# Attention followed by a mixture-of-experts layer: tokens sorted by expert on chip, gathered in slot tiles, and scattered back

## The chip, the core and the metric

The kernel runs on one core of a Trainium2 chip. The metric is the device time of one execution in microseconds (us); lower is better. Five engines work from queues of their own, each in program order: TensorE (PE in the profile; its weight loads are PEld), VectorE (DVE), ScalarE (ACT), GpSimd (POOL), and SyncE (SP), which here only issues transfers. POOL issues transfers too. All transfers share 16 DMA engines.

## What is computed

The reference has two layers. The first is attention with normalised queries and keys, 8 batches x 12 heads, 448 tokens, head size 64. Its output, as rows of 768 numbers, is the input of the second layer: a dense feed-forward network (FFN) for every token, plus the FFN of the one expert of eight that the token's gate picks, weighted by the gate's probability.

```python
x = np.ascontiguousarray(attn_out.transpose(0, 2, 1, 3)).reshape(B * S, H * D)   # 3584 x 768
h_dense = np.maximum(x @ w1_dense, 0.0)          # 768 -> 512
y_dense = h_dense @ w2_dense                     # 512 -> 768
logits = x @ w_gate
expert_idx = np.argmax(logits, axis=1)
probs = softmax(logits)
gate_w = probs[np.arange(N), expert_idx]
for e in range(E):
    mask = expert_idx == e
    h = np.maximum(x[mask] @ w1[e], 0.0)
    y_moe[mask] = gate_w[mask, None] * (h @ w2[e])
return y_dense + y_moe
```

## The kernel before

**Attention** goes over 48 steps t: 8 batches of 6 pairs of heads. The loop at the end of the first `with` block writes the order out by hand. In step t it loads and squares inputs for t+6 (`norm_ahead`, with GP = 3 pairs to one load), normalises t+3, computes `scores` for t+1 and `attend` for t in four parts, transposes the result of t-1 (`xtrans`), transposes q and k of t+2, and ends with `divide(t)`. A step has 52 TensorE instructions of the matmul kind: 8 scores (L137), 32 attend (L150), 8 transposes of q and k (L121) and 4 of the result (L168). ScalarE does the exponentials (`ex`, L139), the copy of the transposed result into `xc` (L170), and once in GP steps `rnorm` (L102 and L103, a logarithm and an exponential), each of which is preceded by a load of its function table. VectorE does the sums of squares (L96), the normalising products (L111), the copies of the transposes (L126, L128) and `divide`. POOL does the squares (L95) and issues the loads of v (`vr`, L84), which VectorE spreads into `va` (L87). SP issues the loads of q and k (L77).

`xc` holds the whole result, transposed (768 numbers of a token lie across partitions), for all 3584 tokens. No token order is changed anywhere.

**The second layer** begins with the gate: 192 matmuls of 8 columns (L220), then a few VectorE operations that leave in `ge` the gate's weight of the chosen expert and zero for the others. Then comes a loop over nine sets of weights: the dense one and the eight experts (e from -1 to 7). The weights `w1t` (L250) and `w2t` (L252) are loaded by POOL into two buffers each. Every set is applied to all 8 batches of 448 tokens: 24 matmuls into `hp` (L258), ScalarE's relu into `ht` (L261), 32 matmuls into `yps` (L267), and VectorE adds the result into `yacc`, multiplied by `ge` (L274; L272 copies for the dense set). An expert thus also runs on the tokens that are not its own, with a factor of zero. With the last expert, the output of a batch is stored as soon as it is complete.

## Time and profile before

| | |
|---|---|
| runs of the kernel before | 1080.33 us median of 3 (1079.74 to 1081.66) |
| the profiled execution | 1080.28 us, its span 1078.2 us |
| instructions | 15442, of them 6720 matmuls |
| busy share of the span | PE 91%, PEld 60%, DVE 47%, ACT 37%, POOL 12% |
| mean granted TensorE clock | 0.911 of full speed |
| moved by the DMA engines | 53.68 MB, mean 50 GB/s |

The span runs from the first to the last instruction. A busy share is a mean over two stages of different kinds, so the stages have to be looked at apart. Matmuls are pipelined: one starts before the record of the previous one ends, so the time of a matmul in a stream is read from a group's length divided by its count, and not from its mean. The granted clock is a share of 2.4 GHz; 0.5 is 1.2 GHz. In the trace, an arrow behind an idle time names what the instruction waited for.

### The profile page before, as it was taken

How to read it: one execution, taken by the hardware profiler on the slowest of the kernel's cores; microseconds unless marked ns; L12 is line 12 of the kernel's file. 1: busy time of each engine (PE TensorE's matmuls, PEld its weight loads, DVE VectorE, ACT ScalarE, POOL GpSimd, SP SyncE). 2: the span in 40 equal slices, each digit the busy share in tenths (PEclk: the TensorE clock that was granted, in tenths of full speed). 3: DMA queues.
4: the chain of work that ended last, by engine and by line, in shares of the span. 5: the costliest groups of instructions: out<-in, count | busy, mean ns of one | idle time of the engine just before them, and what ended most of it. 6: DMA issues, size and time to landing. Idle time of an engine off the chain costs nothing.

```text
span 1078.2 us, 15442 instructions
## 1 busy us (share of the span) xinstructions
PE 985.4 (91%) x6720; PEld 651.4 (60%) x6720; DVE 505.5 (47%) x716; ACT 395.5 (37%) x593; POOL 129.4 (12%) x129
## 2 busy tenths in 40 slices
PE   0579888888897999999999999999999999999996
PEld 0246555555555866666666666666666666666664
DVE  2866657666642333443444334433444344433443
ACT  1577777867765022222222222222222222222221
POOL 4744242342200000000000000000000000000000
PEclk9999956656657699999999999999999999999999
DMA  9964424513000000300300300300301202100334
GB/s 187 195 145 78 105 76 81 125 52 101 3 1 3 1 1 1 59 1 1 60 1 1 59 1 1 59 1 1 59 1 15 45 1 31 29 1 1 121 136 153
DMA packets 46899, 53.68 MB, mean 50 GB/s; under 512 B 2160, under 2 KB 45936, under 8 KB 45936
## 3 DMA queue, kind: packets, MB, share of 16 engines
q0 software_dynamic: 23472, 19.67, 12.7%
q1 hardware_dynamic: 23360, 33.03, 10.7%
q8 instruction: 52, 0.85, 0.3%
q14 instruction: 15, 0.12, 0.0%
HBM read 61.37 MB, written 11.01 MB: 67 GB/s over the span
## 4 chain that ended last, share of the span: by engine, by line
PE 81%; ACT 9%; DMA 4%; DVE 3%; issue 1%; POOL 0%; SPq 0%; ACTq 0%; POOLq 0%; DVEq 0%
PE yps L267 35%; PE hp L258 31%; PE av L150 6%; PE ps L137 6%; ACT ex L139 5%; DMA t<-in_k_dram 3%; PE ps L121 2%; PE lp L220 2%; DVE y L111 2%; PE ps L168 1%; ACT L102 1%; ACT L103 1%; DMA vr<-in_v_dram 1%; DVE ssq L96 1%; ACT xc L170 0%
## 5 line engine op out<-in xcount | busy, mean ns | idle before, releaser
L274 DVE SCALAR_TENSOR_TENSOR yacc<-yps,ge,yacc 112x768 f32<-112x768 f32 x256 | 260.5, 1018 | 362.9 <-PE yps L267 362.9
L267 PE MATMUL yps<-w2t,ht 128*112 128x384 bf16 x2304 | 386.2, 326 | 0.0
L261 ACT ACTIVATE ht<-hp 128x448 bf16<-128x448 f32 x288 | 156.5, 543 | 540.5 <-PE hp L258 540.5
L267 PEld LDWEIGHTS <-ht 128*112 128x112 bf16 x2304 | 299.5, 130 | 81.0
L258 PE MATMUL hp<-xc,w1t 128*128 128x448 bf16 x1728 | 340.7, 354 | 0.0
L258 PEld LDWEIGHTS <-w1t 128*128 128x128 bf16 x1728 | 169.7, 98 | 153.0 <-issue 2.4
L139 ACT ACTIVATE ex<-ps 112x896 bf16<-112x896 f32 x192 | 166.2, 915 | 46.1 <-PE ps L137 45.6
L137 PE MATMUL ps<-y 64*112 64x448 bf16 x384 | 127.3, 551 | 36.2 <-ACT ex L139 35.9
L95 POOL TENSOR_TENSOR sq<-t 112x512 f32<-112x512 f32 x96 | 105.8, 1124 | 141.6 <-DMA t<-in_q_dram 107.5
L150 PEld LDWEIGHTS <-ex 112*128 112x128 bf16 x1536 | 84.0, 123 | 57.3 <-issue 52.8
L150 PE MATMUL av<-va,ex 112*128 112x65 bf16 x1536 | 103.6, 234 | 3.6 <-DVE xa L160 3.6
L121 PE MATMUL ps<-ident,y 112*128 112x112 bf16 x384 | 46.4, 281 | 39.7 <-DVE y L111 33.1
L137 PEld LDWEIGHTS <-y 64*112 64x112 bf16 x384 | 37.8, 160 | 72.9 <-issue 66.6
L96 DVE TENSOR_REDUCE ssq<-sq 112x8 f32<-112x512 f32 x96 | 61.8, 676 | 25.5 <-POOL sq L95 25.2
L111 DVE TENSOR_TENSOR y<-t,r 112x512 bf16<-112x512 f32 x96 | 72.4, 763 | 0.0
L250 POOL DMA_DIRECT2D w1t<-in_moe_w_dram x8 | 6.6, 830 | 527.4 <-PE hp L258 527.4
L121 PEld LDWEIGHTS <-y 112*128 112x128 bf16 x384 | 33.0, 133 | 48.8 <-DVE y L111 35.4
L126 DVE TENSOR_SCALAR y<-ps,gqk 128x448 bf16<-128x448 bf16 x48 | 21.5, 448 | 68.4 <-PE ps L121 68.4
L272 DVE COPY yacc<-yps 112x768 f32<-112x768 f32 x32 | 30.6, 957 | 43.5 <-PE yps L267 43.5
L170 ACT COPY xc<-ps 128x448 bf16<-128x448 bf16 x48 | 25.5, 532 | 26.2 <-PE ps L168 26.1
L160 DVE TENSOR_TENSOR xa<-av,inv 128x512 bf16<-128x512 f32 x48 | 32.8, 684 | 0.2
L168 PE MATMUL ps<-ident,xa 128*128 128x128 bf16 x192 | 27.5, 292 | 1.0 <-DVE xa L160 1.0
(35 smaller groups left out, 165.9 us busy)
## 6 DMA issues: line engine op xcount, KB each, us to landing
t<-in_q_dram SPq DMA_DIRECT2D x16, 672.0 KB, 6.3
t<-in_k_dram SPq DMA_DIRECT2D x16, 672.0 KB, 7.6
out_dram<-yacc SPq DMA_DIRECT2D x8, 1344.0 KB, 6.2
w1t<-in_moe_w_dram POOLq DMA_DIRECT2D x8, 768.0 KB, 7.4
w2t<-in_moe_w_dram POOLq DMA_DIRECT2D x8, 768.0 KB, 9.0
vr<-in_v_dram POOLq DMA_DIRECT2D x8, 672.0 KB, 7.4
w1t<-in_moe_w_dense_dram POOLq DMA_DIRECT2D x1, 768.0 KB, 9.8
w2t<-in_moe_w_dense_dram POOLq DMA_DIRECT2D x1, 768.0 KB, 10.7
```

What stands on the lines that cost most here:

```text
L95: nc.gpsimd.tensor_mul(sq, x, x)
L96: nc.vector.tensor_reduce(ssqs[g][:, n, 2 * i * JJ:(2 * i + 2) * JJ], sq.rearrange("p h (j d) -> p (h j) d", d=D), AX.X, ALU.add)
L111: nc.vector.tensor_mul(y.rearrange("p j h d -> p h j d"), x.rearrange("p h (j d) -> p h j d", d=D), rs[g][:, n, 2 * i * JJ:(2 * i + 2) * J ...
L121: nc.tensor.transpose(ps[:, j * SC:(j + 1) * SC], xn[name, t][:, j].rearrange("p h d -> p (h d)"), ident[:SC, :SC])
L137: nc.tensor.matmul(ps[:, hh, :S], qkT["k", t][d0:d0 + D, j * SC:(j + 1) * SC], qkT["q", t][d0:d0 + D, :], start=True, stop=True)
L139: nc.scalar.activation(exs[t][:, j], ps[:, :, :S], AF.Exp, scale=scale)
L150: nc.tensor.matmul(av[t][:, hh, mi * De:(mi + 1) * De], exs[t][:, j, hh, QC[mi]:QC[mi] + P], vas[b][:, 2 * pr + hh, j, :De], start=(j == 0 ...
L168: nc.tensor.transpose(ps[:, QC[mi]:QC[mi] + P], xnats[t][:, mi].rearrange("p h d -> p (h d)"), ident)
L258: nc.tensor.matmul(hp, w1t[:, kk, ff * P:(ff + 1) * P], xc[:, kk, b * S:(b + 1) * S], start=(kk == 0), stop=(kk == KD - 1))
L261: nc.scalar.activation(ht[:, ff], hp, AF.Relu)
L267: nc.tensor.matmul(yps[:, dd, :HD], ht[:, ff, j * SC:(j + 1) * SC], w2t[:, ff, dd * HD:(dd + 1) * HD], start=(ff == 0), stop=(ff == FT - 1))
L274: nc.vector.scalar_tensor_tensor(yv, in0=yps[:, :, :HD], scalar=ge[:, n, e:e + 1], in1=yv, op0=ALU.mult, op1=ALU.add)
```

## The change

It does four things.

1. **Attention's groups are smaller.** GP goes from 3 to 2, loads run 4 steps ahead in place of 6, v is loaded by groups too, and several tiles have fewer buffers. Before the first instruction of ScalarE one function table is loaded that holds the logarithm and the exponential both (also relu and copy). All nine sets of weights are kept in SBUF and loaded during attention: the dense set with group 1, an expert with each even group from 4 to 18.
2. **Routing moves into attention.** `xTs` holds the transposed rows of one batch alone. After the last pair of a batch, `route(b)` computes the gate (24 matmuls), a one-hot row `oh` for each token, and the gate's probability, which is put behind the token's 768 bf16 numbers; SP stores these rows of 1540 bytes in a DRAM tensor `x_rows`.
3. **Tokens are sorted on chip.** After attention, two matmuls count how many tokens of each expert stand ahead of a token; VectorE works out a slot for each, with each expert's slots starting at a multiple of 128, so that 35 tiles of 128 slots hold any routing (28 tiles of tokens and up to 7 more). 32 matmuls turn the slots into two tables: which row of `x_rows` a slot reads, and which row of the output it writes. Empty slots write nowhere.
4. **35 tiles.** For each, POOL gathers 128 rows by an indirect transfer, two tiles ahead. TensorE transposes them, runs the dense FFN and the FFN of the tile's own expert into one sum (`yp`), and POOL scatters the result's rows into the output. Which expert it is, TensorE reads from SBUF into a register, and the matmuls on `we` take their address from it. The gate's probability enters as the scale of ScalarE's relu.

The core of the diff (setup of small constants, and arithmetic of the same kind as that shown, left out):

```diff
-    GP = 3
+    GP = 2
+    nc.scalar.preload_act_table_set("natural_log_exp_and_others")
-    xcp = ctx.enter_context(tc.tile_pool(name="xc", bufs=1))
-    xc = xcp.tile([P, KD, N], BF16)
...
+    xd = nc.dram_tensor("x_rows", (N, RW // 2), F32).ap()
+    wgb = const.tile([P, KD, E], BF16)
+    nc.gpsimd.dma_start(wgb, moe_w_gate.rearrange("(ko p) e -> p ko e", p=P))
+    wd1 = const.tile([P, KD, F], BF16)
+    wd2 = const.tile([P, FT, Dm], BF16)
+    we = const.tile([P, E, 2, KD * F], BF16)
...
-         tc.tile_pool(name="a_sb", bufs=3) as sb, \
+         tc.tile_pool(name="a_sb", bufs=2) as sb, \
...
+        def load_v(g):
+            b, h0 = divmod(g * GP * 2, H)
+            vr = ld.tile([SC, 2 * GP, JJ * D], BF16, tag="vr", bufs=2)
+            nc.gpsimd.dma_start(vr, v[b, h0:h0 + 2 * GP].rearrange("h (p j) d -> p h (j d)", j=JJ))
+            va = ld.tile([SC, 2 * GP, JJ, D + 2], BF16, tag="va")
...
-            nc.scalar.copy(xc[:, pr, b * S:(b + 1) * S], ps)
+            nc.scalar.copy(xTs[b][:, pr], ps)
+            if pr == NPR - 1:
+                route(b)
+
+        def route(b):
+            lp = trp.tile([P, 4, E], F32, tag="tr")
+            for mi in range(4):
+                for kk in range(KD):
+                    nc.tensor.matmul(lp[:, mi], xTs[b][:, kk, QC[mi]:QC[mi] + P], wgb[:, kk, :],
+                                     start=(kk == 0), stop=(kk == KD - 1))
...
+            nc.vector.reciprocal(xnats[b][:, :, Dm:].bitcast(F32), sm)
+            dst = xd[b * S:b * S + 3 * P].rearrange("(m p) w -> p m w", p=P)
+            nc.sync.dma_start(dst, xnats[b][:, :3].bitcast(F32))
+            nc.sync.dma_start(xd[b * S + 3 * P:(b + 1) * S], xnats[b][D:, 3].bitcast(F32))
...
                 if i == 0:
                     load(g)
-                    if g % 2 == 0:
-                        load_v(t // NPR)
+                    load_v(g)
+                    if g == 1:
+                        load_weights(wd1, wd2, moe_w1_dense, moe_w2_dense)
+                    if g >= 4 and g % 2 == 0 and g // 2 - 2 < E:
+                        load_expert(we[:, g // 2 - 2], g // 2 - 2)
...
+        cp = ps1.tile([P, NC4, E], F32, tag="tr")
+        nc.tensor.matmul(cp.rearrange("p n e -> p (n e)"), tri, ohf, start=True, stop=True)
+        tp = ps2.tile([P, NC4, E], F32, tag="hd")
+        nc.tensor.matmul(tp.rearrange("p n e -> p (n e)"), ones, ohf, start=True, stop=True)
+        tot = one.tile([P, E, NC4], F32)
+        nc.vector.tensor_copy(tot, tp.rearrange("p n e -> p e n"))
+        for e in range(E):
+            nc.vector.tensor_tensor_scan(incl[:, e], onef, tot[:, e], 0.0, ALU.mult, ALU.add)
...
+        sel = one.tile([P, NC4, P], BF16)
+        nc.vector.tensor_tensor(sel, iop.unsqueeze(1).to_broadcast([P, NC4, P]),
+                                lo.unsqueeze(2).to_broadcast([P, NC4, P]), ALU.is_equal)
+        tl = one.tile([P, NC4, NTL], BF16)
+        nc.vector.tensor_tensor(tl, iot.unsqueeze(1).to_broadcast([P, NC4, NTL]),
+                                hi.unsqueeze(2).to_broadcast([P, NC4, NTL]), ALU.is_equal)
+        val = one.tile([P, NC4, 3, NTL], BF16)
+        nc.vector.tensor_tensor(
+            val, tl.unsqueeze(2).to_broadcast([P, NC4, 3, NTL]),
+            tok.rearrange("p b m k -> p (b m) k").unsqueeze(3).to_broadcast([P, NC4, 3, NTL]),
+            ALU.mult)
+        slp = ps2.tile([P, 3, NTL], F32, tag="he")
+        for n in range(NC4):
+            nc.tensor.matmul(slp.rearrange("p k t -> p (k t)"), sel[:, n],
+                             val[:, n].rearrange("p k t -> p (k t)"),
+                             start=(n == 0), stop=(n == NC4 - 1))
...
+        def gather(t):
+            xg = sb.tile([P, RW // 2], F32, tag="xg", name="xg")
+            nc.gpsimd.indirect_dma_start(
+                out=xg, out_offset=None, in_=xd,
+                in_offset=bass.IndirectOffsetOnAxis(ap=row[:, t:t + 1], axis=0))
+            xgs[t] = xg
+
+        def ffn(t):
+            xg = xgs[t]
+            xb = xg[:, :Dm // 2].bitcast(BF16)
+            xp = ps1.tile([P, KD, P], BF16, tag="tr")
+            for kk in range(KD):
+                nc.tensor.transpose(xp[:, kk], xb[:, kk * P:(kk + 1) * P], ident)
+            xT = sb.tile([P, KD, P], BF16, tag="xT")
+            nc.vector.tensor_copy(xT, xp)
+            gate = xg[:, Dm // 2:]
+            ereg = nc.tensor.value_load(tei[:, t:t + 1], min_val=0, max_val=E - 1)
+            he = ps2.tile([P, F], F32, tag="he")
+            for kk in range(KD):
+                nc.tensor.matmul(he, xT[:, kk], we[:, bass.ds(ereg, 1), 0, kk * F:(kk + 1) * F].rearrange("p o f -> p (o f)"), start=(kk == 0), stop=(kk == KD - 1))
+            hs = sb.tile([P, F], BF16, tag="hs")
+            nc.scalar.activation(hs, he, AF.Relu, scale=gate)
+            hd = ps2.tile([P, FT, P], F32, tag="hd")
+            for ff in range(FT):
+                for kk in range(KD):
+                    nc.tensor.matmul(hd[:, ff], wd1[:, kk, ff * P:(ff + 1) * P], xT[:, kk],
+                                     start=(kk == 0), stop=(kk == KD - 1))
+            hdT = sb.tile([P, FT, P], BF16, tag="hdT")
+            nc.scalar.activation(hdT, hd, AF.Relu)
+            hp = ps1.tile([P, FT, P], BF16, tag="tr")
+            for ff in range(FT):
+                nc.tensor.transpose(hp[:, ff], hs[:, ff * P:(ff + 1) * P], ident)
+            heT = sb.tile([P, FT, P], BF16, tag="heT")
+            nc.vector.tensor_copy(heT, hp)
+            yp = psy.tile([P, 2, 512], F32, tag="y")
+            for ff in range(FT):
+                for dd in range(2):
+                    nc.tensor.matmul(yp[:, dd, :HD], hdT[:, ff], wd2[:, ff, dd * HD:(dd + 1) * HD],
+                                     start=(ff == 0), stop=False)
+            for ff in range(FT):
+                for dd in range(2):
+                    nc.tensor.matmul(yp[:, dd, :HD], heT[:, ff], we[:, bass.ds(ereg, 1), 1, ff * Dm + dd * HD:ff * Dm + (dd + 1) * HD]
+                                     .rearrange("p o f -> p (o f)"),
+                                     start=False, stop=(ff == FT - 1))
+            ys = sb.tile([P, 2, HD], F32, tag="ys")
+            nc.vector.tensor_copy(ys, yp[:, :, :HD])
+            nc.gpsimd.indirect_dma_start(
+                out=out, out_offset=bass.IndirectOffsetOnAxis(ap=dest[:, t:t + 1], axis=0),
+                in_=ys.rearrange("p a d -> p (a d)"), in_offset=None,
+                bounds_check=N - 1, oob_is_err=False)
+
+        for t in range(2):
+            gather(t)
+        for t in range(NTL):
+            if t + 2 < NTL:
+                gather(t + 2)
+            ffn(t)
```

## Rows read from the trace of the kernel before

**Rows 1.** The chain that ended last, share of the span by line (page part 4).

```profile
PE yps L267 35%; PE hp L258 31%; PE av L150 6%; PE ps L137 6%; ACT ex L139 5%; DMA t<-in_k_dram 3%; PE ps L121 2%; PE lp L220 2%; DVE y L111 2%; PE ps L168 1%; ACT L102 1%; ACT L103 1%; DMA vr<-in_v_dram 1%; DVE ssq L96 1%; ACT xc L170 0%
```

**Rows 2.** The same chain in order of time: start us, length us, what.

```profile
373.05 5.20 PE yps L267 x32
378.25 4.54 PE hp L258 x24
...
1064.59 5.21 PE yps L267 x32
```

**Rows 3.** Stretches: length, busy by engine (instructions), granted clock, DMA share, GB/s.

```profile
130.00:180.00 50.00, 41.27 (x416) 26.19 (x414) 33.28 (x66) 39.75 (x52) 17.92 (x18) 0.65 0.50 107
280.00:330.00 50.00, 43.74 (x404) 26.77 (x402) 23.30 (x51) 33.98 (x44) 0.00 (x0) 0.57 0.00 1
400.00:480.00 80.00, 80.00 (x461) 53.17 (x459) 31.35 (x32) 18.47 (x34) 1.57 (x2) 1.00 0.14 20
```

**Rows 4.** The timeline: start us, length us, what, [idle before <- releaser].

```profile
174.44 0.40 PE L137 MATMUL ps<-y 64*112 64x448 bf16 x2 [2.64 <-ACT ex L139]
...
342.57 0.67 PE L150 MATMUL av<-va,ex 112*128 112x65 bf16 x16
...
343.52 0.69 DVE L160 TENSOR_TENSOR xa<-av,inv 128x512 bf16<-128x512 f32 x1
...
344.26 0.40 PE L168 MATMUL ps<-ident,xa 128*128 128x128 bf16 x4 [1.03 <-DVE xa L160]
344.70 0.53 ACT L170 COPY xc<-ps 128x448 bf16<-128x448 bf16 x1 [1.40 <-PE ps L168]
...
348.41 18.05 PE L220 MATMUL lp<-wgb,xc 128*112 128x8 bf16 x192 [3.75 <-DMA wgb<-in_moe_w_gate_dram]
```

**Rows 5.** Groups by line: | busy us, mean ns of one | idle before us <- releasers.

```profile
L267 PE MATMUL yps<-w2t,ht 128*112 128x384 bf16 x2304 | 386.2, 326 | 0.0
...
L139 ACT ACTIVATE ex<-ps 112x896 bf16<-112x896 f32 x192 | 166.2, 915 | 46.1 <-PE ps L137 45.6
L261 ACT ACTIVATE ht<-hp 128x448 bf16<-128x448 f32 x288 | 156.5, 543 | 540.5 <-PE hp L258 540.5
...
L272 DVE COPY yacc<-yps 112x768 f32<-112x768 f32 x32 | 30.6, 957 | 43.5 <-PE yps L267 43.5
...
L102 ACT ACT_TABLE_LOAD x16 | 20.5, 1283 | 1.0 <-PEq L293 0.7
L128 DVE COPY y<-ps 128x448 bf16<-128x448 bf16 x48 | 18.6, 388 | 6.8 <-PE ps L121 6.7
...
L103 ACT ACT_TABLE_LOAD x14 | 18.0, 1283 | 0.2
...
L84 POOL DMA_DIRECT2D vr<-in_v_dram x8 | 8.0, 998 | 16.7 <-DVE va L87 16.3 <-issue 0.4
...
L240 DVE TENSOR_TENSOR ge<-hot,left 112x32 f32<-112x32 f32 x8 | 1.7, 217 | 0.3
```

**Rows 6.** DMA queues: packets, MB, share; issues: KB each, us to landing.

```profile
q0 software_dynamic: 23472, 19.67, 12.7%
q1 hardware_dynamic: 23360, 33.03, 10.7%
...
w2t<-in_moe_w_dense_dram POOLq DMA_DIRECT2D x1, 768.0 KB, 10.7
...
wgb<-in_moe_w_gate_dram POOLq DMA_DIRECT2D x1, 12.0 KB, 2.6
```

**Rows 7.** The timeline of SP, an issue of a q load.

```profile
37.26 0.31 SPq L77 DMA_DIRECT2D t<-in_q_dram  x1
```

**Rows 8.** Stretches of 2 us, columns as in rows 3.

```profile
212.00:214.00 2.00, 1.31 (x15) 0.84 (x15) 0.31 (x1) 2.00 (x4) 1.04 (x1) 0.86 0.80 200
342.00:344.00 2.00, 1.24 (x36) 1.11 (x32) 0.69 (x2) 0.53 (x1) 0.00 (x0) 1.00 0.00 0
346.00:348.00 2.00, 0.00 (x0) 0.00 (x0) 0.00 (x0) 0.00 (x0) 0.18 (x1) 0.64 0.57 6
```

More of the change, by code (lines that the diff above doesn't have):

```diff
@@ new lines @@
+    col = const.tile([P, 4], F32)
+    for mi in range(4):
+        nc.gpsimd.iota(col[:, mi:mi + 1], pattern=[[0, 1]], base=QC[mi], channel_multiplier=1,
+                       allow_small_or_imprecise_dtypes=True)
+    cmp3 = const.tile([P, 4, JJ - 1], F32)
+    for jj in range(1, JJ):
+        nc.vector.tensor_scalar(cmp3[:, :, jj - 1], col, float(jj * SC), None, op0=ALU.is_ge)
+    colj = const.tile([P, 4], F32)
+    nc.vector.tensor_reduce(colj, cmp3, AX.X, ALU.add)
+    colp = const.tile([P, 4], F32)
@@ new lines @@
+    nc.vector.scalar_tensor_tensor(colp, in0=colj, scalar=-float(SC), in1=col,
+                                   op0=ALU.mult, op1=ALU.add)
+    tok = const.tile([P, B, 4, 3], BF16)
+    for b in range(B):
+        nc.vector.memset(tok[:, b, :, 0], float(b + 1))
+        nc.vector.tensor_copy(tok[:, b, :, 1], colj)
+        nc.vector.tensor_copy(tok[:, b, :, 2], colp)
+    nc.vector.memset(tok[:D, :, 3, :], 0.0)
+    xd = nc.dram_tensor("x_rows", (N, RW // 2), F32).ap()
+    oh = const.tile([P, B, 4, E], BF16)
@@ L132, in scores @@
             if j == 0:
-                exs[t] = sb.tile([SC, JJ, 2, S], BF16, tag="ex", name="ex")
+                exs[t] = sb.tile([SC, JJ, 2, S], BF16, tag="ex", name="ex", bufs=2)
             ps = scp.tile([SC, 2, 512], F32, tag="sc")
@@ new lines @@
+        nc.vector.scalar_tensor_tensor(t1, in0=sl[:, 1], scalar=float(SC), in1=sl[:, 2],
+                                       op0=ALU.mult, op1=ALU.add)
+        nc.vector.tensor_add(t1, t1, bs)
+        row = one.tile([P, NTL], I32)
+        nc.vector.tensor_scalar(row, t1, 0.0, None, op0=ALU.max)
+        t2 = one.tile([P, NTL], F32)
+        nc.vector.scalar_tensor_tensor(t2, in0=sl[:, 2], scalar=float(JJ), in1=sl[:, 1],
+                                       op0=ALU.mult, op1=ALU.add)
+        nc.vector.tensor_add(t2, t2, bs)
```

190 lines of the change are left out of this document (110 added, 80 removed).

## The prediction, made before the changed kernel was run

> **What bounds the kernel now.** I read the chain of waits first, by line, then in order of time [rows 1, 2]. Two lines of the second layer, hp (L258) and yps (L267), make 66% of the chain. They alternate without a gap: 24 hp matmuls of 448 columns in 4.54 us, 32 yps matmuls of 384 columns in 5.20 us, one such pair for each of 8 batches and 9 weight sets, 72 pairs. The table by stretches says the same of that stage: TensorE busy 80 of 80 us, granted clock 1.00, the DMA engines at 0.14 [rows 3]. It is bound by matmul columns alone; only less work there can shorten it. Attention is another regime: TensorE is busy 83 to 87%, but at a mean granted clock of 0.57 to 0.65 [rows 3]. The last attention copy ends at 344.70 + 0.53 = 345.2 us [rows 4], so what comes behind attention takes 1078.2 - 345.2 = **733 us**.
>
> **The change, part by part.** The second layer goes from 9 x 3584 token passes to 35 tiles of 128 slots with two passes each. I price one tile, the handover, attention and the tail.
>
> *One tile, TensorE's own work.* The two rows give 0.189 us for 448 columns and 0.1625 us for 384, or 0.42 ns a column at full clock. Six he matmuls of 512 columns: 1.30 us. Sixteen yp of 384: 2.60. Twenty-four hd and ten transposes of 128 columns: 34 x 0.055 = 1.87. Sum 5.77 us. Weight loads fit beside them: 16 matmuls of 65 columns with 128-column weights took 0.67 us, some 0.03 us each behind the first one's latency [rows 4].
> A rule speaks against the 0.055. The Trainium skill (TensorE: Matmul & The Clock Gate, Back-to-back issue gap) gives 81 ns for a 128-column matmul in a stream with weight loads; by it, as an estimate, a tile takes 0.9 us more and the total 31 us more. No run here shows that floor: the row with 0.03 us for each pair speaks against it, and I keep 0.055.
>
> *One tile, waits.* TensorE works in program order, so two waits stay open in each tile. (a) The transposes of tile t+1 need a VectorE copy (xT), and that stands in VectorE's queue behind tile t's output copy ys. ys has the shape of L272's, 0.957 us. A small op costs 0.217 (L240, 32 elements), so the slope is 1.0 ns an element; for bf16 from PSUM, L128's 388 ns gives 0.45 ns, and xT of 768 columns takes 0.53 [rows 5]. A matmul's record runs 0.16 us past its issue time (L267's mean 326 less 162.5 ns), and a hand-over took 0.05 (xa's end at 344.21 to the transposes at 344.26) [rows 4, 5]. So 0.16 + 0.05 + 0.96 + 0.05 + 0.53 + 0.05, less six transposes that run meanwhile (0.33): **1.47 us**. (b) The dense half of yp waits for ScalarE's hdT: from L261 and L139 0.83 ns a column, so 512 columns take 0.60; 0.16 + 0.05 + 0.60 + 0.05 - 0.22 (four transposes) = **0.64 us**. hs runs beside hd, heT beside (b). A tile is 5.77 + 1.47 + 0.64 = 7.88 us, 35 of them **276 us**.
>
> *Costed at nothing in a tile.* Gather and scatter on POOL: the trace of before has no indirect DMA. A POOL trigger took 1.0 us (L84), landings 2.6 (wgb) to 10.7 us (w2t) [rows 5, 6]. I take 1.0 plus about 3; two of them hide in 7.9 us, and the gather runs two tiles ahead. If POOL were held until the landing, see the last rival. The register load and the 14 addresses made from it (six he, eight yp) run on TensorE's sequencer. Nothing like it is in the trace; the nearest sequencer step is an SP issue at 0.31 us [rows 7], so 0 to 15 x 0.31 = 4.7 us. It is covered by the 2.60 us of yp already queued and the 1.47 us of wait (a), and I take 0; the most under that cover is 0.6 us a tile.
>
> *Handover, nothing of it hidden.* From the last attention copy: twenty route matmuls 1.0, seven small VectorE ops 1.5, two 256-column matmuls 0.5. Then VectorE alone: seven ops of 256 to 280 elements at 0.45 and five shorter ones at 0.2 to 0.4, eight scans and five small ops at 0.217, and the three wide ones, sel (4096 elements, 4.3 us), tl (1120, 1.3) and val (3360, 3.6), 16.8 in all. Then 32 matmuls at the half-clock price of the gate matmuls (18.05/192 = 0.094 [rows 4]), 3.0; row arithmetic 1.2; trigger and landing of the first gather 3.6. Sum **28 us**, bounds 20 (sel and val at bf16 copy speed) to 36 (gather landing at 10.7).
>
> *Attention.* Gone are the table loads: 1.28 us each, 16 at L102, 14 at L103, 38.5 us of ScalarE [rows 5]. What reaches TensorE is less: where a pair of them stands between two exps, TensorE shows one gap of 2.64 us [rows 4], and there are five such gaps. I take 18 us, ends 0 and 38.5. Added is route() once a batch: TensorE waits for an xT copy queued behind up to two exps of 0.915, so 0.6 to 2.0 us, then 24 small matmuls, 0.7 to 2.3 us by the rates above; I take 2.3 x 8 = 18 us, ends 10 and 34. VectorE's ten small ops go beside it. The two take each other off.
> SP's queue now holds the store of x rows, which waits for route(), ahead of the next q and k loads; these are needed a step later, so 0. The weights are loaded during attention: by queue shares [rows 6] POOL's transfers cost 137 us / 19.67 MB = 7.0 us a MB, SP's 3.5. Between steps 4 and 32, 8 experts (10.9 us each), 14 groups of q, k and v (4.8) and 4.7 stores (2.4) make 166 us of 16 engines. A step has 52 matmuls, so 404 in 50 us [rows 3] are 6.4 us a step, 28 steps 179 us. It just fits; v, queued behind an expert on POOL's ring, may come late for VectorE's copy: 0 to 20 us, taken 0. The prologue loads smaller groups, but two dense matrices and some 30 tiny constant ops stand ahead: 0, ends -10 and +10. Attention: **0**, ends -38 and +54.
>
> *Tail.* After the last ys a trigger and a landing: 5 us.
>
> *Sum.* 28 + 276 + 5 = 309 in place of 733: 424 less. 1078.2 - 424 = 654.2, and 2.1 us lie around the span of this execution (1080.28), which stands at the median of the runs (1080.33): **656 us**.
>
> **The rivals.**
> *The clock falls between tiles.* Before, it fell from 1.00 to 0.50 behind each of the five gaps of 2.64 us (a mean of 0.86 in 212:214) and in the 3.75 us wait for wgb (0.64 in 346:348), yet stayed at 1.00 through 342:344 with TensorE busy 1.24 of 2 us [rows 4, 8]. Wait (a), 1.47 us behind transposes, lies between. If it falls there and comes back within each tile, he and hd (2.62 us) run at half speed: 10.5 us a tile, 748 us. Never coming back: 5.77 us more a tile, less 0.55 hidden in the waits, 839. Against it stands the 342:344 stretch, emptier than any tile: TensorE works 5.77 of a tile's 7.88 us. 15%. The Trainium skill (TensorE: Matmul & The Clock Gate, HAM oscillation) tells of a kernel with M = 128, as these tiles have, at 25.9% of peak because its clock fell in the wait of every K-tile; the gaps of 2.64 us here agree with such a fall, and no row shows it for a wait of 1.5 us.
> *TensorE's sequencer.* If the register steps find no cover: 4.7 x 35 = 163 more, 819; half of it, 737. 10%.
> *Attention grows* by late v and the route waits, up to its end of 54: 710. For it: the DMA engines are 93% filled over 28 steps (166 of 179 us). 9%.
> *Slower.* POOL's queue becomes the bound: gather and scatter alternate on it, and if each holds POOL until it lands, at w2t's 10.7 us, a tile takes 21.4 and the stage 749: 28 + 749 + 5 = 782 against 733, 1129 us. It decides from (733 - 33)/35 = 20.0 us a tile. Against it: POOL went on issuing within 1.0 us in the trace. 3%.
> That it does nothing is hardly possible, since all 35 tiles are written out whatever the routing gives; 1% that sizes meet within 0.2%, which is about what a measurement of this kernel tells from no change.
>
> **How the numbers follow.** Forecast 62%, on its own 622 to 712. The range 610 to 750 leaves out half of the clock case, the uncovered sequencer, the slow case and a few per cent below. Faster 0.96, same 0.01, slower 0.03.
>
> **What would show it.** Right: tiles 7.9 us apart, granted clock near 1.00 there, two TensorE waits a tile (on xT and hdT), hd near 55 ns each, attention ending within 345 +- 30 us, some 28 us to the first tile. Wrong: a clock of 0.5 to 0.8 in the tile stage, he waiting for the sequencer, scatter or gather as releaser, or VectorE's va copy waiting for vr in attention.

## The result, and the profile after

The changed kernel takes **606.95 us** (median of 4 runs, 599.36 to 609.44) against 1080.03 us of the kernel before (1079.71 to 1081.66): a ratio of 0.5579, 95% interval 0.5526 to 0.5633. The ratio is taken over executions in the faster of the program's two states alone (602.8 us on average), so it is not the quotient of the medians. The forecast was 656 us in a range of 610 to 750. The direction was right, and 473 us less where 424 were forecast; but the time lies 3 us below the range.

The profiled execution took 599.36 us, its span is 597.7 us where the sum gave 654.2. I cut that span where the prediction cut it:

| part | forecast | measured | difference |
|---|---|---|---|
| attention, to the end of the last xT copy | 345.2 | 314.71 + 0.53 = 315.2 | -30.0 |
| handover, to the first transposes of a tile | 28 | 352.05 - 315.24 = 36.8 | +8.8 |
| 35 tiles, to the end of the last ys copy | 276 | 239.7 | -36.3 |
| tail | 5 | 5.9 | +0.9 |

The table by stretches of the changed kernel, in the columns of [rows 3]:

```profile
352.00:360.00 8.00, 7.12 (x48) 5.09 (x49) 1.12 (x3) 1.28 (x2) 1.37 (x2) 0.54 0.23 62
130.00:180.00 50.00, 42.61 (x465) 27.72 (x465) 37.86 (x81) 35.14 (x54) 22.52 (x23) 0.62 0.57 126
280.00:310.00 30.00, 25.11 (x368) 16.56 (x366) 18.00 (x46) 25.35 (x37) 0.00 (x0) 0.93 0.08 25
400.00:480.00 80.00, 71.36 (x671) 48.59 (x672) 22.72 (x36) 15.04 (x24) 23.29 (x24) 1.00 0.23 75
```

The first line is the first tile, still at half the clock after the empty handover. The second answers to its namesake of before: about the same clock in mid-attention, but more matmuls. The third is the end of attention, at 0.93 where 280 to 330 us of before had 0.57. The last is the tile stage: the clock is at 1.00 throughout, and TensorE is no longer busy all the time: 8.6 of 80 us are waits.

The handover in the timeline of the changed kernel (start, length, what, idle before and releaser):

```profile
314.71 0.53 ACT L229 COPY xT<-ps 128x448 bf16<-128x448 bf16 x1 [1.41 <-PE ps L227]
...
317.46 0.42 PE L310 MATMUL tp<-oh,ones 128*128 128x256 bf16 x1
...
321.43 0.42 DVE L312 COPY tot<-tp 128x256 f32<-128x256 f32 x1 [4.18 <-DMA x_rows<-xa]
...
333.36 3.65 DVE L364 TENSOR_TENSOR val<-tl,tok 128x3360 bf16<-128x3360 bf16 x1
...
343.65 2.98 PE L370 MATMUL slp<-val,sel 128*128 128x105 bf16 x32 [25.76 <-issue]
...
348.82 1.06 POOL L397 DMA_INDIRECT xg<-x_rows,row  x1 [70.63 <-DVE dest L390]
...
352.05 0.82 PE L407 MATMUL xp<-ident,xg 128*128 128x128 bf16 x6 [5.42 <-DMA xg<-x_rows,row]
```

Two gaps stand in it that the prediction doesn't have. The copy of tot waits 4.18 us for the store of token rows, which it doesn't read. And slp starts 6.64 us after its last operand is complete (333.36 + 3.65 = 337.01); "issue" says that no releaser is seen. The rest has the lengths of the forecast: sel and tl 4.42 and 1.32 us (forecast 4.3 and 1.3), val 3.65 (3.6), slp 2.98 (3.0), and from the first gather's trigger to its rows 3.2 us (3.6).

Two tiles in a row, a common one and one of the four short ones:

```profile
446.16 0.27 PEld L426 LDWEIGHTS <-hs 128*128 128x128 bf16 x4
446.22 0.39 PE L426 MATMUL hp<-ident,hs 128*128 128x128 bf16 x4
446.34 0.98 POOL L397 DMA_INDIRECT xg<-x_rows,row  x1 [0.30 <-issue]
...
446.44 0.50 PE L407 MATMUL xp<-ident,xg 128*128 128x128 bf16 x6
447.11 0.42 DVE L428 COPY heT<-hp 128x512 bf16<-128x512 bf16 x1 [2.38 <-PE xp L407]
447.11 0.60 ACT L423 ACTIVATE hdT<-hd 128x512 bf16<-128x512 f32 x1 [1.30 <-PE xp L407]
...
447.77 1.48 PE L432 MATMUL yp<-wd,hdT 128*128 128x384 bf16 x8 [0.83 <-issue]
447.85 0.56 DVE L409 COPY xT<-xp 128x768 bf16<-128x768 bf16 x1 [0.31 <-PE xp L407]
...
450.58 0.96 DVE L440 COPY ys<-yp 128x768 f32<-128x768 f32 x1 [2.17 <-PE yp L436]
...
451.67 1.50 PE L420 MATMUL hd<-xT,wd 128*128 128x128 bf16 x24
...
453.01 0.39 PE L426 MATMUL hp<-ident,hs 128*128 128x128 bf16 x4
...
453.27 0.60 ACT L423 ACTIVATE hdT<-hd 128x512 bf16<-128x512 f32 x1 [0.66 <-PE hd L420]
...
453.66 0.98 POOL L397 DMA_INDIRECT xg<-x_rows,row  x1 [0.83 <-issue]
...
453.93 1.47 PE L432 MATMUL yp<-wd,hdT 128*128 128x384 bf16 x8 [0.19 <-ACT hdT L423]
```

First: the next tile's transposes (xp, L407) stand **ahead** of yp on TensorE, and their copy xT ahead of ys on VectorE. The code has them the other way round; the program that builds the queues has moved them. So wait (a) is gone. Second: TensorE's own work is as forecast. The 24 hd start at 451.67, hp at 453.01: 0.056 us each (forecast 0.055). The 81 ns of the Trainium skill (TensorE: Matmul & The Clock Gate, Back-to-back issue gap) are not seen in this stream with its weight loads. Third: in the common tile hdT starts at 447.11, 0.95 us after the last hd matmul (446.16); in the short one 0.31 us after it (452.96 to 453.27). In 30 tiles TensorE so waits some 0.83 us for hdT, in the other five (the first and the four short ones) 0.19; a later tile takes 6.78 or 6.16 us. An idle time counts from the modelled end of the last matmul, some 0.16 us later than the issue that the prediction counts from: in its count the wait is 0.36 us in the short tile, and TensorE's own work 6.16 - 0.36 = 5.80 us.

The lateness lies ahead of ScalarE. The trace's records of semaphore updates have TensorE's signal behind hd 0.85 to 0.90 us after the start of the last hd matmul in the 30 tiles and 0.23 us in the short ones. (As it comes after xp's modelled end, the profile names xp, and not hd, as what hdT and heT waited for.) Whether the matmul itself ended late or only its signal can't be told from these rows, since matmul ends are modelled.

### The profile page after: what moved, and what is told of

It is laid out like the page before. It is cut to its first block, busy times and chain, and to the rows that moved or that the text cites. A ratio compares the mean times of both kernels' runs of the same rounds, so it can differ in the third digit from the quotient of the medians.

```text
span 597.7 us, 11804 instructions
## 1 busy us (share of the span) xinstructions
PE 443.1 (74%) x4682; PEld 294.6 (49%) x4682; DVE 311.6 (52%) x666; ACT 247.4 (41%) x367; POOL 205.7 (34%) x223
## 4 chain that ended last, share of the span: by engine, by line
DMA 31%; issue 26%; PE 17%; DVE 15%; POOL 4%; ACT 4%; SPq 1%; POOLq 0%; DVEq 0%; ACTq 0%
DMA out_dram<-ys,dest 16%; DMA vr<-in_v_dram 7%; PE av L206 7%; DMA t<-in_k_dram 5%; PE ps L193 5%; DVE y L167 4%; ACT ex L195 4%; POOL sq L151 3%; PE ps L177 2%; DVE xa L219 2%; DMA t<-in_q_dram 2%; DVE ssq L152 2%; PE ps L227 2%; DVE va L143 1%; POOL xg L397 1%
## 5 line engine op out<-in xcount | busy, mean ns | idle before, releaser
L193 PE MATMUL ps<-y 64*112 64x448 bf16 x384 | 98.3, 493 | 41.9 <-DVE y L184 25.9
L441 POOL DMA_INDIRECT out_dram<-ys,dest x35 | 35.5, 1016 | 158.7 <-DVE ys L440 158.7
L440 DVE COPY ys<-yp 128x768 f32<-128x768 f32 x35 | 33.5, 958 | 77.4 <-PE yp L436 77.4
L432 PE MATMUL yp<-wd,hdT 128*128 128x384 bf16 x280 | 51.6, 327 | 25.8 <-ACT hdT L423 20.0
L397 POOL DMA_INDIRECT xg<-x_rows,row x35 | 34.2, 977 | 86.3 <-DVE dest L390 70.6
L420 PEld LDWEIGHTS <-wd 128*128 128x128 bf16 x840 | 51.1, 99 | 8.6 <-issue 0.6
L420 PE MATMUL hd<-xT,wd 128*128 128x128 bf16 x840 | 53.9, 222 | 0.0
L414 PE MATMUL he<-we,xT 128*128 x210 | 52.3, 386 | 0.8 <-DVE xT L409 0.8
L436 PE MATMUL yp<-we,heT 128*128 x280 | 51.2, 326 | 0.0
L432 PEld LDWEIGHTS <-hdT 128*128 128x128 bf16 x280 | 24.5, 98 | 45.3 <-ACT hdT L423 24.6
```

The source lines that it names most:

```text
L193: nc.tensor.matmul(ps[:, hh, :S], qkT["k", t][d0:d0 + D, j * SC:(j + 1) * SC], qkT["q", t][d0:d0 + D, :], start=True, stop=True)
L397: nc.gpsimd.indirect_dma_start(out=xg, out_offset=None, in_=xd, in_offset=bass.IndirectOffsetOnAxis(ap=row[:, t:t + 1], axis=0))
L414: nc.tensor.matmul(he, xT[:, kk], we[:, bass.ds(ereg, 1), 0, kk * F:(kk + 1) * F].rearrange("p o f -> p (o f)"), start=(kk == 0), stop=(kk ...
L420: nc.tensor.matmul(hd[:, ff], wd1[:, kk, ff * P:(ff + 1) * P], xT[:, kk], start=(kk == 0), stop=(kk == KD - 1))
L432: nc.tensor.matmul(yp[:, dd, :HD], hdT[:, ff], wd2[:, ff, dd * HD:(dd + 1) * HD], start=(ff == 0), stop=False)
L436: nc.tensor.matmul(yp[:, dd, :HD], heT[:, ff], we[:, bass.ds(ereg, 1), 1, ff * Dm + dd * HD:ff * Dm + (dd + 1) * HD] .rearrange("p o f -> ...
```

## The experiments

Line numbers in the rows are those of each edited kernel. `chain(...)` and `pin` stand for an edge that keeps an instruction behind the previous one of its queue. Kernels that ran one after the other on one chip form a series (a "call" in the expectations): experiments 1 to 4 (e1_order to e4_own); 5 to 8 (e5_spread to e8_gp3); e9_after to e12_best; and e13_lponly to e16_double. Experiments 1 to 4 and e7_before_preload are single executions, so they are read by stretches of their traces more than by their run times. The attention's code is the same in the changed kernel and in seven of the profiled experiments (1 to 4, e9_after, e12_best, e15_after); it ended between 312.5 and 319.8 us in these eight, so a difference of a few us in this end is no effect of an edit.

**1. The order on the queues** (e1_order). All matmuls, transposes and copies of the tiles are kept as written.

```diff
             ffn(t)
+            chain(n0, ("InstMatmult", "InstTensorCopy"))
```

> The slot tiles' matmuls and transposes on TensorE, and the copies on VectorE, are kept in the order in which they are written: a tile's transposes stand behind the yp matmuls of the tile before, and its xT copy behind that tile's ys copy. Theory (the tile stage came out 36 us shorter than forecast because the builder moved the next tile's transposes and their copy ahead of yp and ys): the two waits of the forecast are both there, TensorE waits for the xT copy 1.3 to 1.6 us in each tile, the tile takes 7.5 to 8.3 us instead of the 6.71 of the changed kernel, the stage from the first transposes to the last ys copy 265 to 285 us instead of 239.7, the run 630 to 655 us. Rival (the order has nothing to do with it, the wait was hidden by something else): the tile stays at 6.6 to 6.9 us, the wait for xT under 0.3 us.

Measured: 637.67 us, stage 281.0 us, a tile 7.92 us. Its waits in 365 to 560 us (total us, times, longest):

```profile
PE he L425 <- DVE xT L420: 31.8, 25, 1.3
...
PE yp L443 <- ACT hdT L434: 12.6, 24, 0.5
```

Both waits of the prediction are there, and with them its tile: 7.88 us forecast, 7.92 measured. (The waits of 1.27 and 0.53 us are 1.43 and 0.69 in the prediction's count; it had 1.47 and 0.64.) In this kernel hdT is not late: the gather's trigger begins some 0.08 us ahead of the last hd matmul (426.92), and hdT starts 0.32 us after it.

```profile
426.84 0.97 POOL L408 DMA_INDIRECT xg<-x_rows,row  x1 [1.81 <-ACT hs L427]
...
427.24 0.60 ACT L434 ACTIVATE hdT<-hd 128x512 bf16<-128x512 f32 x1 [0.66 <-PE hd L431]
```

The reordering is worth 281.0 - 239.7 = 41 us, and against the 220.9 us of experiment 2, where no signal is late either, 60 us.

**2. The gather's place** (e2_gather). Released by the xT copy, it stands ahead of the scatter of the tile before.

```diff
+            pin(nc.gpsimd.tensor_copy(tick, xT[:1, 0, :1]))
+            if t + 2 < NTL:
+                gather(t + 2)
+            if t > 0:
+                scatter(t - 1)
...
-            if t + 2 < NTL:
-                gather(t + 2)
```

> The gather two tiles ahead is released by the xT copy (through a one-element GpSimd copy that reads it) and stands ahead of the scatter of the tile before, so that it is triggered while TensorE is in the yp matmuls and no longer at the end of hd. Theory (while GpSimd works on a gather's trigger, TensorE's signals that a matmul has finished arrive late, and ScalarE starts hdT 0.6 us late): hdT starts 0.2 to 0.35 us after hd's last matmul in all tiles, TensorE waits 0.1 to 0.3 us for hdT instead of 0.8, the tile takes 6.05 to 6.25 us instead of 6.78 in 30 of 35 tiles, the stage 214 to 222 us instead of 239.7, the run 575 to 592 us. Rival (the late signal has another cause, and gather and signal only begin together): the stage stays within 236 to 243 us.

Measured: 580.1 us, stage 220.9 us, all tiles 6.16 us (one 6.44).

```profile
438.34 0.60 ACT L432 ACTIVATE hdT<-hd 128x512 bf16<-128x512 f32 x1 [0.66 <-PE hd L429]
...
438.99 1.47 PE L441 MATMUL yp<-wd,hdT 128*128 128x384 bf16 x8 [0.19 <-ACT hdT L432]
...
440.23 1.00 POOL L399 DMA_INDIRECT xg<-x_rows,row  x1 [0.52 <-DMA out_dram<-ys,dest]
```

With the trigger at 440.23, in the middle of yp, no hdT is late, while the two other kernels of the same series that leave the gather where it was (3 and 4) have it late, with stages of 239.6 and 239.4 us. Moving it gives 19 us. But the theory as put is too simple: in e1_order a trigger is under way at hd's end without harm, and 5, 6 and 8 have it at the old place without harm: see 9.

**3. The register loads** (e3_loads). The trace's records of TensorE's sequencer show what stood behind "issue": 23 of the 35 loads of an expert's number, moved ahead of slp, one after the other from 326.5 to 342.5 us, 0.70 us each. The view of the tile that they read (durations in ns, first and last start):

```profile
L411 PEldq TENSOR_LOAD <-tei x35: 295/299/496, 326.5 to 357.9; - x35
```

```diff
+        eregs = [nc.tensor.value_load(tei[:, t:t + 1], ...) for t in range(14)]
...
+        with tc.issue_after(slm.ins):
+            for t in range(14, 25):
+                eregs.append(nc.tensor.value_load(tei[:, t:t + 1], ...))
...
+            m = turn(t + 1)      # transposes and xT of the next tile
+            with tc.issue_after(m.ins):
+                eregs.append(nc.tensor.value_load(tei[:, u:u + 1], ...))
```

> Of the 35 register loads on TensorE's queue, 14 stay ahead of slp, 11 are put behind it, and 10 go one to a tile, behind the next tile's transposes, where TensorE waits for hdT anyway. Theory (nine of the 23 loads that stood ahead of slp held it back): slp starts within 1 us after the val multiplication has ended, instead of 6.6, the first gather is triggered 5.5 to 7 us earlier against the end of attention (26.5 to 28.1 us behind the last xT copy instead of 33.6), and the tiles do not change: 6.5 to 6.8 us each. The run 595 to 604 us. Rival (the loads come back on the path behind slp or in the tiles): the first transposes start under 3 us earlier, or the ten tiles with a load take over 0.3 us more than the others.

Measured: 594.51 us. In the timeline slp now follows its operand:

```profile
334.31 3.65 DVE L367 TENSOR_TENSOR val<-tl,tok 128x3360 bf16<-128x3360 bf16 x1
338.50 2.98 PE L373 MATMUL slp<-val,sel 128*128 128x105 bf16 x32 [19.63 <-DVE val L367]
```

It starts 0.54 us after val's end, the first gather 27.4 us after the last xT copy (33.6 in the changed kernel), the first transposes 31.0 (36.8): 5.8 us won. The ten tiles with a load take 6.73 to 6.81 us, like the others, so a load there is hidden.

**4. Tables in memory of their own** (e4_own). The changed kernel lays them over the attention's buffers.

```diff
+    tab = ctx.enter_context(tc.tile_pool(name="m_tab", bufs=1))
...
-        tot = one.tile([P, E, NC4], F32)
+        tot = tab.tile([P, E, NC4], F32)
```

and so for 16 other small tables.

> The small tables of the routing between attention and tiles (tot, incl and what comes of them) lie in memory of their own and not over the attention's buffers. Theory (the tot copy waits for the last store of token rows to land, only because it lies over the buffer that the store reads): tot's copy starts 0.2 to 0.8 us after the tp matmul, VectorE's wait of 4.2 us for the store is gone, and the first gather's trigger comes 3.5 to 4.3 us earlier against the last xT copy (29.2 to 30.1 us behind it instead of 33.6). The run 595 to 606 us. Rival (another wait takes its place, or slp, held by the register loads, eats it): under 1.5 us earlier.

Measured: 592.97 us.

```profile
315.19 0.42 PE L312 MATMUL tp<-oh,ones 128*128 128x256 bf16 x1
...
315.65 0.42 DVE L314 COPY tot<-tp 128x256 f32<-128x256 f32 x1 [0.68 <-PE tp L312]
```

The wait for the store is gone, the first gather comes 29.8 us after the last xT copy, 3.8 us earlier.

**5. Weights spread over the attention** (e5_spread, e10_spread2). In the changed kernel the builder moved all expert loads forward, to 34 to 98 us: the DMA engines are over-full until 130 us (a share of 1.18 in 80 to 130), and VectorE's copy of v waits for its load three times. Waits of 30 to 315 us (total us, times, longest):

```profile
DVE va L143 <- DMA vr<-in_v_dram: 12.8, 3, 5.6
```

```diff
-        nc.gpsimd.dma_start(dst1, s1.rearrange("(ko p) f -> p ko f", p=P))
+        tc.keep_in_program_order(nc.gpsimd.dma_start(dst1, s1.rearrange("(ko p) f -> p ko f", p=P)))
```

and likewise for the second matrix.

> The triggers of the weight loads are kept where they are written on GpSimd's queue (one expert to every second group of pairs) instead of being moved forward to 34 to 98 us. Theory (the packed weight loads crowd out the v loads behind them and cost the attention time in 30 to 135 us): the DMA share of 80 to 130 us falls from 1.18 to under 0.85, that of 130 to 230 us rises from 0.5 to 0.7 or more, more than 430 matmuls on PE in 80 to 130 us instead of 375, the last xT copy ends at 292 to 306 us instead of 315.2, the run 580 to 598 us. Rival (TensorE gives it back: what is gained early is lost by a lower clock later, or the squares that stand behind the triggers on GpSimd now wait): the last xT copy ends at 311 to 322 us, the run 597 to 612 us.

> The kernel of e5_spread (weight loads in program order on GpSimd's queue) once more, beside the changed kernel on one chip, since e5's attention of 328.3 us was read on another chip than the changed kernel's 315.2. Theory (the spread loads cost the attention time: TensorE's clock is lower or squares wait behind triggers): the last xT copy ends 8 to 15 us later than in e9_after. Rival (the two chips differ, the spread itself gains or is neutral): the last xT copy ends within 5 us of that of e9_after, or earlier.

Measured: 590.9 us (584.72 to 596.93, 4 runs) in one series, with the attention's end at 328.3 us; in the other 608.04 (602.76 to 610.78) beside 600.53 (596.62 to 602.61) of the changed kernel, with the ends at 317.4 and 312.6. The same stretch of e9_after and of e10_spread2:

```profile
80.00:130.00 50.00, 33.41 (x391) 21.89 (x389) 32.72 (x74) 29.49 (x44) 21.34 (x23) 0.71 1.18 238
```

```profile
80.00:130.00 50.00, 40.08 (x435) 25.63 (x431) 36.08 (x81) 33.50 (x49) 24.11 (x27) 0.62 0.85 170
```

The DMA share falls from 1.18 to 0.85 and more matmuls are done here, as the theory has it, but it is given back: from 130 to 230 us the clock is at 0.56 and 0.54 (0.68 and 0.66 without the edit), and all in all 7.5 us are lost. In the second series the end and the run lie where the rival of e5_spread put them (311 to 322 and 597 to 612 us); its theory of a gain falls. The loss of attention that e10_spread2 expected (8 to 15 us) is not shown: 4.8 us are less than its rival's 5, and less than the spread of the unedited attention. In the first series the same program ended its attention 11 us later than in the second, outside both forecasts; what made the difference is open.

**6 and 7. The table loads** (e6_tables, e7_before_preload). One line, taken out of the changed kernel and put into the kernel before.

```diff
-    nc.scalar.preload_act_table_set("natural_log_exp_and_others")
```

> The line that loads one activation table for the whole kernel is left out, so that ScalarE loads a table at each change between Ln and Exp again: with 24 groups up to 48 loads of 1.28 us, 61 us in all, instead of one. Theory (the forecast's 18 us for 30 loads, 0.6 us each on the path): the attention's end moves from 315.2 to 335 to 350 us, the run 622 to 645 us. Rival A (the loads were hidden behind other work): the attention's end moves by less than 6 us. Rival B (every load is on the path): the end at 365 us or later.

> The kernel before, with the one line that loads the activation table once added to it. Theory (the 30 table loads cost 18 us, as forecast): 1060 to 1066 us, with the last exp of the attention 14 to 20 us earlier than 338. Rival (they were hidden): 1077 to 1082 us. If all of the 30 us by which the attention became shorter come from the tables: 1048 to 1053 us.

Measured: without it 621.96 us (620.42 to 622.28), 48 table loads where there was one, and the attention ends at 355.9 us, 40.7 later than in the changed kernel's own profile and 36 to 43 later than in the eight; that is above the theory's 350 and below the 365 of rival B. The run grows by less than that beside the median of the changed kernel, because the tiles of e5 to e8 were short (219.6 us, see 9). Put into the kernel before, it gives 1053.52 us (one execution; 1079.4 without), and the last copy of the attention in its timeline,

```profile
318.57 0.53 ACT L171 COPY xc<-ps 128x448 bf16<-128x448 bf16 x1 [1.40 <-PE ps L169]
```

ends at 319.1 us where [rows 4] give 345.2: 26.1 us for 31 loads fewer (the trace of before has 32, with two at L139 that the forecast left out), 0.84 us of each 1.28. The changed kernel agrees within its spread (36 to 43 us for 47 loads, 0.77 to 0.92). The forecast's 18 us were too little: the five gaps of 2.64 us on TensorE were only where it shows most, and 5.3 us stand ahead of TensorE's first transposes, which start at 27.75 us with the line and at 33.06 without. But the granted clock changed with the edit too (230 to 280 us: 0.69 with the line, 0.57 without), so how much of the 26.1 us is ScalarE's time and how much came back through the clock is not shown.

**8. The groups** (e8_gp3). Three pairs to a group, as before.

```diff
-    GP = 2
+    GP = 3
...
-                    if g >= 4 and g % 2 == 0 and g // 2 - 2 < E:
-                        load_expert(we[:, g // 2 - 2], g // 2 - 2)
+                    if g >= 3 and g - 3 < E:
+                        load_expert(we[:, g - 3], g - 3)
```

> The changed kernel with groups of three pairs of heads, as before, instead of two (one expert's weights to each group from the fourth on). Theory (the first transposes came 13 us earlier because the first group of q and k is a third smaller): the first transposes start at 29 to 34 us instead of 19.9, the attention ends at 324 to 332 us, the run 612 to 625 us. Rival (the earlier start comes from the table loads that are gone from the beginning, and from other changes): the first transposes start at 19 to 24 us, the run 595 to 610 us.

Measured: the first transposes start at 28.7 us, 8.8 later than in the changed kernel and nearly as the theory has it, but the attention ends at 315.9 us, within the spread of the changed kernel; 589.48 us (581.37 to 600.71), with the short tiles of e5 to e8 (220.8 us). So 8.8 of the 13 us of an earlier start (33.06 to 19.90) belong to the groups. They look like a gain in the timeline, and are given back before the end.

**9. The changed kernel again** (e9_after, e15_after), because 5, 6 and 8 had shown short tiles with the gather at its old place.

> The changed kernel itself once more, beside three others on one chip, because its tile stage took 239.7 us in its own profile and 219.6 to 220.8 in three kernels with other attentions but the same tile code, where the gather's trigger began at the same place, 0.18 us after the last hd matmul, and hdT was not late. So the simple form of the theory of e2_gather has fallen: the trigger alone does not make the signal late. Theory A (it takes the trigger and something that belongs to the chip or the core that a run is on): in this call the stage of this kernel, of e10_spread2 and of e11_noroute is the same in all three, near 220 us or near 240 us. Theory B (it belongs to the program): this kernel shows 239 to 241 us again and e10_spread2 shows 220 us.

> The changed kernel as the base of this call: the last xT copy at 310 to 317 us, the run 596 to 609 us if the late signals of e9_after are there (tile stage near 240 us), 577 to 590 us if not (near 220).

Measured: 600.53 us and 601.46 us (597.46 to 615.18), stages of 239.8 and 239.7 us. In e9's series e10_spread2 has 241.1 us, while the identical program, e5_spread, had 220.6 on a chip with the same number. In e5_spread the trigger stands at the same place, 0.18 us after the last hd matmul (451.20), but hdT is not late:

```profile
451.38 0.98 POOL L397 DMA_INDIRECT xg<-x_rows,row  x1 [0.30 <-issue]
...
451.52 0.60 ACT L423 ACTIVATE hdT<-hd 128x512 bf16<-128x512 f32 x1 [0.66 <-PE hd L420]
```

So theory B is out; theory A holds if "chip" is read as the series: within a series the profiled kernels with the gather at its old place agree. Both are needed, a trigger that begins right behind hd (moved away, it leaves the signals on time in e2_gather and in e12_best, in series where the others have them late) and a condition from outside the program. What that is stays open; that the recording of a profile has a part in it can't be excluded either.

**10. The price of the route** (e11_noroute, e13_lponly, e14_chainonly, e16_double). For seven of eight sequences all of it, or its chain of small operations, or 20 of its 24 matmuls are left out, or the matmuls are doubled. The first three no longer compute the layer: seven sequences go by a fixed expert or by logits of a sixth of the sum. The 35 tiles run all the same.

```diff
+            if b < B - 1:                                  # e11; e13: behind the lp matmuls
+                nc.vector.memset(oh[:, b], 0.0)
+                nc.vector.memset(oh[:, b, :, b:b + 1], 1.0)
+                nc.vector.memset(xnats[b][:, :, Dm:].bitcast(F32), 1.0)
+                store(b)
+                return
...
-                for kk in range(KD):
+                for kk in (KD - 1,):                       # e14, b < B - 1
+                for kk in list(range(KD)) * 2:             # e16
```

> For the first seven of eight sequences the routing is left out (the logits, their maximum, the softmax sum and the one-hot): the one-hot names a fixed expert, the gate is 1; the eighth keeps it. So 168 of 192 lp matmuls and seven of eight chains on VectorE and ScalarE are gone from the attention. Theory (the route that the change put into the attention costs the 18 us that the forecast gave it, but other savings hid that): the last xT copy ends 13 to 20 us earlier than in e9_after. Rival (the route fills waits and costs the path little, which is why the attention became shorter by more than forecast): under 6 us earlier.

> For the first seven of eight sequences the 24 lp matmuls stay, but what comes of them (maximum, softmax sum, one-hot on VectorE and ScalarE) is left out, with a fixed one-hot and a gate of 1. Theory (the clock is what sets the attention's second half, and the small matmuls, which bring TensorE pauses in front of them, are what held it up): the last xT copy ends within 5 us of e15_after's, with a clock of 0.62 or more over 180 to 310 us. Rival (the chain holds TensorE back, and with it the clock up): it ends 10 us or more later, the clock under 0.56.

> For the first seven of eight sequences 4 of the 24 lp matmuls stay and all of the chain. Mirror image of e13_lponly: by the theory that the matmuls hold the clock up, the last xT copy ends 10 us or more later than in e15_after with a clock under 0.56 over 180 to 310 us; by the rival (the chain does), within 5 us of it and 0.62 or more. If neither of the two is enough by itself, or the builder's new order of the attention is the cause, both e13_lponly and e14_chainonly end 10 us later.

> Each of the lp matmuls is done twice, 384 instead of 192. By the forecast's price (18 us for eight routes, most of it their matmuls and the wait before them) the last xT copy ends 5 to 10 us later than in e15_after. By the theory (the route fills pauses, and its matmuls hold the clock up): not later than 3 us, or earlier.

The clock is the one that the stretch of 180 to 310 us shows:

| kernel | route | run, us | attention's end | clock |
|---|---|---|---|---|
| e9_after (base) | whole | 600.53 (596.62 to 602.61) | 312.6 | 0.80 |
| e11_noroute | none | 612.19 (611.34 to 613.35) | 328.4 | 0.53 |
| e15_after (base) | whole | 601.46 (597.46 to 615.18) | 319.5 | 0.71 |
| e14_chainonly | a sixth of the matmuls | 603.85 (602.13 to 606.12) | 318.4 | 0.70 |
| e16_double | twice the matmuls | 619.71 (615.88 to 622.01) | 336.5 | 0.58 |

Two of these stretches, of e9_after and of e11_noroute:

```profile
180.00:310.00 130.00, 100.92 (x1319) 66.90 (x1319) 92.11 (x219) 95.41 (x139) 41.55 (x42) 0.80 0.40 93
```

```profile
180.00:310.00 130.00, 119.48 (x1092) 74.89 (x1092) 86.44 (x185) 87.52 (x123) 42.65 (x44) 0.53 0.41 94
```

Without the route TensorE has fewer matmuls to do, is busy for longer with them, and gets a lower clock: leaving work out costs 12 us of run time. So the theory of e11_noroute (13 to 20 us earlier) falls. Taking out most of the matmuls alone (e14_chainonly) neither gains nor loses, so the theory that the small matmuls hold the clock up falls too. By the letter of its rival it would be the chain of small operations, but e13_lponly, which was to show that, settles nothing: its four runs lie between 607.07 and 621.41 us, the profiled one among the long ones. A second set of the matmuls costs 18 us of run and 17 of attention, more than either side of e16_double had expected; that this is the price which the forecast had put on the whole route is chance.

By and large the end is later where the clock is lower, but e16_double ends after e11_noroute at a higher one. Whether the clock sets the length, or an attention held up otherwise is granted the lower clock, these runs do not separate. Which part of the route is at work, or whether it is the new order that the builder makes of the attention with each edit, stays open.

**11. The edits that held, together** (e12_best): 2, 3 and 4.

> The three edits that held, together: the gather released by the xT copy, the register loads spread, the small routing tables in memory of their own. Expected against e9_after of the same call: the first transposes of a tile 9 to 10.5 us earlier behind the last xT copy (26.5 to 28 us instead of 36.8), the tile stage 219 to 223 us, whatever the chip does to e9_after's; the attention unchanged. The run 10 us faster than e9_after if that one's stage is near 220 us, 29 us faster if it is near 240. If the edits get into each other's way, for instance the loads and the gathers in the first tiles, under 6 us faster.

Measured: **575.6 us** (572.82 to 578.24), ratio to the kernel before 0.5336 (0.5312 to 0.5361), where e9_after on the same chip has 0.5572 (0.5557 to 0.5587). Its timeline from the last xT copy on:

```profile
319.23 0.53 ACT L231 COPY xT<-ps 128x448 bf16<-128x448 bf16 x1 [1.62 <-PE ps L229]
...
322.43 0.42 DVE L314 COPY tot<-tp 128x256 f32<-128x256 f32 x1 [0.68 <-PE tp L312]
...
338.25 2.99 PE L375 MATMUL slp<-val,sel 128*128 128x105 bf16 x32 [15.86 <-DVE val L369]
...
347.02 0.82 PE L418 MATMUL xp<-ident,xg 128*128 128x128 bf16 x6 [5.79 <-DMA xg<-x_rows,row]
```

The first transposes come 27.3 us after the attention, 9.4 sooner than in e9_after (36.6), the stage takes 220.2 us, 19.6 less. That is 29 us, as expected. The two profiled executions differ by 21.7, as the attention of e12_best, at a clock of 0.66 over 180 to 310 us, ended 7.2 us later than that of e9_after; the medians differ by 24.9.

## Why the prediction missed, point by point

- **The step that failed** is "TensorE works in program order, so two waits stay open in each tile", with its term (a): 1.47 us x 35 = 51 us, measured as nothing. It is not the mechanism of the waits that is wrong, since e1_order shows both and a tile of 7.92 us, but what the queues hold: they need not have the order of the code. Without (a), wait (b) shrinks too, since six more transposes run beside hdT: from 0.64 to 0.36 us in the prediction's count, 10 us in all. The late signals put 0.62 us on 30 tiles, some 19 us, which nothing in the trace of before announced. The first tile takes 11.4 us to the end of its ys copy, most of it at half the clock, 5 more than a short one. With 1 us for TensorE's own work, -51 - 10 + 19 + 5 + 1 = -36 us, the difference measured.
- **TensorE's own 5.77 us** a tile were right: 5.80 in the same count, with hd at 0.056 us each.
- **Attention, forecast 0, measured -30** (-25 to -33 by the eight profiles). Two terms of 18 us were to take each other off, and both were mis-sized. Without its table loads the attention of the kernel before is 26.1 us shorter (e7), 8 more than taken, inside the ends of 0 to 38.5. The route's 18 us were not to be had back by leaving it out (e11): in the attention as it stands it shows no price, below the bound of 10. Taken so, the two make 26 of the 30 us. Both were measured where the granted clock moved as well; over 180 to 310 us it is 0.59 in the kernel before and 0.75 in the changed one. How much of the 30 us goes back to the clock, and what raised it, is not shown.
- **Luck.** Wait (a) alone would bring the forecast from 656 to 605 us, close to what was measured. The other misses (attention -30, wait (b) -10, late signals +19, handover +9, first tile +5, the rest +2) come to -5 us in the profiled execution: they cancel, and no reasoning made them do so.
- **The DMA engines** do fill up (a share of 1.18 in 80 to 130 us), as the rival of a growing attention had it, but earlier than planned, since the builder moved the loads forward; there is time to make it good later, and the attention did not grow. One of the signs of being wrong that the prediction names did show: VectorE's va copy waited for vr, 12.8 us in all (experiment 5).
- **Handover, forecast 28, measured 36.8.** The arithmetic was right: without the two gaps it is 27.3 (e12). They were missed: memory that the new tables share with a buffer still being stored (3.8 us, e4), and register loads gathered ahead of the last matmuls (5.8 us, e3). The prediction had looked for the sequencer's price in the tiles, where it is hidden.
- **The rivals.** The clock did not fall between tiles: 1.00 over 400 to 480 us, with a wait of 0.83 us in most, and also in e1_order, whose waits have the size that the rival was made for. The fall that the Trainium skill describes (TensorE: Matmul & The Clock Gate, HAM oscillation) is not seen here. GpSimd was held 0.98 to 1.06 us by an indirect transfer, not until it landed, so the slower case had no ground.
- **The range** should have reached lower: its low end counted on (a) in every tile, an order that nobody had read from the queues.

## What to carry to other kernels

A wait that follows from the order of the code is a forecast of the queue's order, so give it a case of its own in which the order is changed, with the whole term at nothing. Where two stages meet, ask of each new buffer whose memory it takes over, and of each queue what is ready early and may stand in front of the last thing that the next stage needs. In a stretch where the granted clock moves, do not count on getting a price in busy time back: work left out made this attention longer.

## What was not expected of the hardware

- A TensorE signal that arrives late: its own record 0.85 to 0.94 us after the start of the last hd matmul instead of 0.23, and hdT 0.94 us after it instead of 0.32, in tiles where the gather's trigger begins 0.18 us after that matmul; not where it begins 0.08 us before it, 0.71 us after it or in yp, and in one of four series not at all.
- A register load on TensorE takes 0.70 us of its sequencer, 35 of them some 24 us; it cost nothing where TensorE waited anyway (ten tiles of e3_loads).
- The table loads of 1.28 us cost 0.84 us each, in run time and not only in ScalarE's, in an attention in which ScalarE, loads included, is busy 80% of the time (39.75 of 50 us, [rows 3]); a part of that may be the clock's.
